# Two matrix mixes in one program: the second mix also takes the first one's banks and tiles in the last ten steps

## The chip, the cores and the metric

The kernel runs on one core of a Trainium2 chip. The core's engines work side by side, each through its own queue, in order: TensorE (PE; its weight loads are listed as PEld), VectorE (DVE), ScalarE (ACT), GpSimd (POOL), and SyncE (SP), which here issues the DMAs. Matrix products land in PSUM, which the kernel uses as eight tiles of 128 x 512 floats, called banks below; everything else lies in SBUF. The metric is the device time of one execution in microseconds (us).

## What is computed

Three layers on an input of 2 batch rows x 4160 tokens x 192 channels, all in 32-bit floats, cut to what matters:

```python
w = softmax(weight_gen)                          # 8 heads, 7 taps
x = einsum('bshk,bskhg->bshg', w, windows(x))    # causal window of 7 tokens
# first mix ("moe"): 192 -> 1024 -> 192
xk = mu_k * x + (1 - mu_k) * x_prev
xr = mu_r * x + (1 - mu_r) * x_prev
k = maximum(xk @ w_k, 0)
x = sigmoid(xr @ w_r) * ((k * k) @ w_v)
# second mix ("moe2"): 192 -> 1024 -> 192
h = maximum(x @ w_in, 0)
conv = sum over k of conv_w[k] * h shifted by k - 1    # 3 taps along the tokens
out = (h * sigmoid(conv)) @ w_out
```

## The kernel before

The tokens are cut into ten tiles (`SIZES`: 256, 248, seven of 472, and 352), and a tile is worked on for both batch rows. The hidden width of 1024 is cut into `NF = 8` chunks of 128, which stand on the partitions. Channels 0 to 127 and 128 to 191 are kept in two parts, and each operand as a high and a low part, so that a product of full accuracy is made of five matmuls.

**A step of the first mix** (`moe1`) is one chunk of one tile and batch row: five matmuls into a bank `pa`, Relu and Square in place, a high part copied to `s` (ACT), the low part (DVE), and five matmuls with `wv` that add up in the banks `am` and `ar`. When the eight chunks are done, `mix_out` multiplies by the gate and writes the result to `x2[b]`, the second mix's input.

**A step of the second mix** (`moe2`, L623) is, for one chunk:

- `go`: five matmuls of `x2[b]` with `wiA` and `wiB` into a bank `pc` (5 passes of N + 2 columns);
- `c1`: Relu from the bank to a tile `h` (ACT); `c2`: `h` times the middle tap back into the bank (ACT);
- two taps on DVE, each a SCALAR_TENSOR_TENSOR that adds to the bank; `c5`: Sigmoid in the bank (ACT); `c6`: `h` times the bank into the bank (DVE), called the product;
- `c7`: the high part from the bank to a tile `g` (ACT); `c8`: the low part, bank minus high part, to `g` (DVE);
- `go2`: five matmuls of `g` with `wo` that add up in `bm` and `br`, called the sums. After chunk 7, `store` copies `bm` to `om` and a part of `br` to `ob` (ACT), adds the rest on DVE, and sends both out.

**Who has how many buffers.** Two banks each for `pa` and `pc`, one each for `am`, `ar`, `bm`, `br`: all eight. Two tiles each of `s`, `g`, `h`, and of `mk`, which the blending with the previous token uses (`mixing`). A `Ring` hands its tiles out in turn. A step of the second mix holds its bank from `go` to `c8`, `h` from `c1` to `c6`, and `g` from `c7` to `go2`.

**What sets the order.** Each piece of work is recorded with a due time (`at`): tile i starts at T = 16 i, batch row 1 eight later, `moe1` of chunk fi at T + fi, and `moe2` ten (`LAG`) behind it. `Program.schedule` (L99) plays the recorded operations through, with the costs of `cost` (L72): at each moment an engine takes, of the operations whose inputs and buffers are ready, the one with the earliest due time. The instructions are then issued in the order of the starts so found. A ring's choice is made before, in the order of the due times, so that a buffer is bound to a step when the step is recorded, and a reuse becomes a dependence that the order obeys. The first mix's last step is due at 159 to 160.25, the second mix's last one at 169.5 to 171.75.

In the trace all instructions bear one line (L167), since `schedule` issues them all; operations are told apart by tile names and by engine. The last tile has 352 tokens; its second mix works on 354 or 356 columns.

Of the kernel before, what the change touches and what calls it, by code (L numbers as in the profile page):

```python
# [16 lines left out]
NTILE = len(SIZES)  # L17
# [7 lines left out]
WIN = KS * DM  # L25
NF = DFF // 128
LAG = 10


def f(ap):  # L30
    return ap.bitcast(F32)


class Program:
# [3 lines left out]
    def __init__(self, nc):  # L38
        self.ops, self.spaces = [], {}
        self.real = {"PE": nc.tensor, "ACT": nc.scalar, "DVE": nc.vector, "POOL": nc.gpsimd, "SP": nc.sync}  # L40
# [129 lines left out]
class Ring:  # L170
# [5 lines left out]
    def __call__(self):  # L176
        self.n += 1
        return self.tiles[(self.n - 1) % len(self.tiles)]
# [3 lines left out]
def conv_moe_kernel(ctx: ExitStack, tc: tile.TileContext, xp, wg_first, wg_rest, mus, w_k, w_v, w_r, w_in, conv_w, w_out, out):  # L182
    nc = tc.nc
    prog = Program(nc)
# [4 lines left out]
    def new(name, shape, dtype=F32):  # L189
        t = sb.tile(shape, dtype, name=name)  # L190
        prog.spaces[t.tensor.name] = "SBUF"
        return t

    def ring(name, n, shape, dtype=F32):
        return Ring([new(f"{name}{j}", shape, dtype) for j in range(n)])

    def bank(name):
        t = ps.tile([128, 512], F32, name=name)
        prog.spaces[t.tensor.name] = "PSUM"
        return t  # L200

    W = NMAX + 4

    mu = new("mu", [128, 4])
    onemu = new("onemu", [128, 4])
    cw = new("cw", [128, 3, NF])
# [21 lines left out]
    mk_r = ring("mk", 2, [128, NMAX])  # L228
# [4 lines left out]
    s_r = ring("s", 2, [128, 2, NMAX], F32R)  # L233
    g_r = ring("g", 2, [128, 2, W], F32R)
    h_r = ring("h", 2, [128, W])
# [14 lines left out]
    pa_r = Ring([bank(f"pa{j}") for j in range(2)])  # L250
    pc_r = Ring([bank(f"pc{j}") for j in range(2)])
    am_r, ar_r, bm_r, br_r = (Ring([bank(x)]) for x in ("am", "ar", "bm", "br"))

    px_r = Ring([bm_r.tiles[0], br_r.tiles[0]])
    py_r = Ring(pc_r.tiles)

    plan = []

    def at(t, fn, hold=0.0):
        plan.append((t, len(plan), fn, hold))  # L260

    def mm(dst, passes):
        n = len(passes)
        for i, (w, r) in enumerate(passes):
            PE.matmul(dst, lhsT=w, rhs=r, start=(i == 0), stop=(i == n - 1))
# [262 lines left out]
    def moe1(i, b, fi, t):  # L528
        N = SIZES[i]
        st = {}  # L530
        sl = slice(128 * fi, 128 * fi + 128)

        def go():
            p = pa_r()
            st["p"] = p[:, :N]
            mm(st["p"], passes_in(wkA, wkB, xin[i, b, 0, 0], xin[i, b, 0, 1], sl, N))

        def c1():
            ACT.activation(st["p"], st["p"], ACTF.Relu)

        def c2():
            ACT.activation(st["p"], st["p"], ACTF.Square)

        def c3():
            s = s_r()
            st["s"] = s
            ACT.copy(s[:, 0, :N], st["p"])

        def c4():
            s = st["s"]  # L550
            DVE.tensor_tensor(s[:, 1, :N], st["p"], f(s[:, 0, :N]), op=ALU.subtract)

        def go2():
            if fi == 0:
                acc["m"] = am_r.tiles[0]
                acc["r"] = ar_r.tiles[0]
            out_passes(wv, fi, st["s"], N, acc["m"], acc["r"])

        at(t, go)
        at(t + 0.28, c1)  # L560
        at(t + 0.45, c2)
        at(t + 0.56, c3)
        at(t + 0.68, c4)
        at(t + 1.25, go2)

    def out_passes(W, fi, s, n, am, ar):
        s0, s1 = s[:, 0, :n], s[:, 1, :n]
        a, z = fi == 0, fi == NF - 1
        PE.matmul(am[:, :n], lhsT=W[:, fi, 0], rhs=s0, start=a, stop=False)
        PE.matmul(am[:, :n], lhsT=W[:, fi, 1], rhs=s0, start=False, stop=False)  # L570
        PE.matmul(ar[:, :n], lhsT=W[:, fi, 2], rhs=s0, start=a, stop=False)
        PE.matmul(am[:, :n], lhsT=W[:, fi, 0], rhs=s1, start=False, stop=z)
        PE.matmul(ar[:, :n], lhsT=W[:, fi, 2], rhs=s1, start=False, stop=z)
# [13 lines left out]
    def mix_out(i, b, t):  # L587
        N = SIZES[i]
        X = x2[b]
        c = slice(2, N + 2)  # L590
        m, r = am_r.tiles[0], ar_r.tiles[0]

        def d0():
            DVE.tensor_tensor(m[:, :N], r_t[0][:, :N], m[:, :N], op=ALU.mult)

        def d1():
            DVE.tensor_tensor(r[:, :N], r_t[1][:, :N], r[:, :N], op=ALU.mult)

        def a0():
            ACT.copy(X[:, 0, c], m[:, :N])  # L600

        def a1():
            ACT.copy(X[:, 2, c], r[:, :N])
            ACT.copy(X[0:64, 3, c], r[0:64, :N])

        def d2():
            DVE.tensor_tensor(X[:, 1, c], m[:, :N], f(X[:, 0, c]), op=ALU.subtract)

        def d3():
            DVE.tensor_tensor(X[64:128, 3, c], r[0:64, :N], f(X[0:64, 2, c]), op=ALU.subtract)  # L610

        at(t, d1)
        at(t + 0.14, d0)
        at(t + 0.15, a1)
        at(t + 0.3, a0)
        at(t + 0.4, d3)
        at(t + 0.5, d2)
# [5 lines left out]
    def moe2(i, b, fi, t):  # L623
        last = i == NTILE - 1
        N = SIZES[i] + (2 if last else 0)
        X = x2[b]
        st = {}
        sl = slice(128 * fi, 128 * fi + 128)

        def go():  # L630
            p = pc_r()
            st["p"] = p
            n = N + 2
            mm(p[:, :n], [(wiA[:, 0, sl], X[:, 0, :n]), (wiA[:, 1, sl], X[:, 0, :n]), (wiA[:, 0, sl], X[:, 1, :n]),
                          (wiB[:, 0, sl], X[:, 2, :n]), (wiB[:, 1, sl], X[:, 3, :n])])

        def c1():
            h = h_r()
            st["h"] = h
            ACT.activation(h[:, :N + 2], st["p"][:, :N + 2], ACTF.Relu)  # L640

        def c2():
            ACT.activation(st["p"][:, :N], st["h"][:, 1:N + 1], ACTF.Copy, scale=cw[:, 1, fi:fi + 1])

        def tap(k, o):
            DVE.scalar_tensor_tensor(out=st["p"][:, :N], in0=st["h"][:, o:o + N], scalar=cw[:, k, fi:fi + 1],
                                     in1=st["p"][:, :N], op0=ALU.mult, op1=ALU.add)

        def c5():
            ACT.activation(st["p"][:, :N], st["p"][:, :N], ACTF.Sigmoid)  # L650

        def c6():
            DVE.tensor_tensor(st["p"][:, :N], st["h"][:, 1:N + 1], st["p"][:, :N], op=ALU.mult)

        def c7():
            g = g_r()
            st["g"] = g
            ACT.copy(g[:, 0, :N], st["p"][:, :N])

        def c8():  # L660
            g = st["g"]
            DVE.tensor_tensor(g[:, 1, :N], st["p"][:, :N], f(g[:, 0, :N]), op=ALU.subtract)

        def go2():
            if fi == 0:
                acc2["m"] = bm_r()
                acc2["r"] = br_r()
            out_passes(wo, fi, st["g"], N, acc2["m"], acc2["r"])

        at(t + 0.5, go)  # L670
        at(t + 0.78, c1)
        at(t + 0.9, c2)
        at(t + 1.03, lambda: tap(0, 0))
        at(t + 1.17, lambda: tap(2, 2))
        at(t + 1.35, c5)
        at(t + 1.47, c6)
        at(t + 1.66, c7)
        at(t + 1.8, c8)
        at(t + 2.75, go2)

    def store(i, b, t):
        N = SIZES[i]
        last = i == NTILE - 1
        a = 1 if i == 0 else 0
        n = N + (1 if last else 0)
        t0 = STARTS[i] - 1
        st = {}

        def e0():
            st["b"] = ob_r()  # L690
            ACT.copy(st["b"][:, :n], acc2["r"][64:128, :n])

        def e1():
            st["m"] = om_r()
            ACT.copy(st["m"][:, :n], acc2["m"][:, :n])
            SP.dma_start(out=out[b, 0:128, t0 + a:t0 + n], in_=st["m"][:, a:n])

        def e2():
            DVE.tensor_tensor(st["b"][:, :n], acc2["r"][0:64, :n], st["b"][:, :n], op=ALU.add)
            SP.dma_start(out=out[b, 128:192, t0 + a:t0 + n], in_=st["b"][:, a:n])  # L700

        at(t, e0)
        at(t + 0.1, e1)
        at(t + 0.2, e2)
# [36 lines left out]
    for i in range(NTILE):  # L741
# [6 lines left out]
        for b in range(NB):  # L748
# [4 lines left out]
            for fi in range(NF):  # L753
                moe1(i, b, fi, t + fi)
                moe2(i, b, fi, t + fi + LAG)
            mix_out(i, b, t + 8.52)
            store(i, b, t + LAG + 10.02)

# [68 lines left out]
```

## Time and profile before

| | us |
|---|---|
| median of 3 runs | 791.23 (789.27 to 791.41) |
| the profiled execution | 793.36 |
| its span, first to last instruction | 791.6 |
| busy in the span: PE, DVE, ACT, POOL | 697.2, 631.4, 666.5, 506.2 |

PE is busy 88% of the span, and the share is not even: in the middle of the program PE is full, at both ends it isn't. An engine's busy time by itself doesn't tell what bounds a stretch. Read by stretch instead which engine is full there, and, where none is, who waits for whom. In the rows below a timeline gives start and duration of an instruction, and in brackets how long its engine was idle before it and what ended that. The duration runs to the end of the result; the next instruction of the same engine can start before that, so an engine's pace is read from the starts of neighbours.

### The profile page before, as it was taken

The page shows a single profiled execution, that of the slowest core. Times are in us where ns is not written, and L with a number is a line of the kernel's source. Part 1 is how long each engine was busy: PE and PEld are TensorE (multiplying, and loading weights), DVE is VectorE, ACT ScalarE, POOL GpSimd, SP SyncE. Part 2 cuts the span into 40 slices and gives each one's busy share as a digit, 9 for nine tenths or more (in the row PEclk, how much of TensorE's full clock was granted, in tenths as well). Part 3 has the DMA queues.
Part 4 walks back from the last instruction along what each step waited for, and adds up shares of the span by engine and source line. Part 5 has one row for each costly group of instructions (what it writes and reads, how often), then busy time and mean ns, then how long its engine had stood idle before and what let it go on. Part 6 is the DMA issues. An engine that isn't in the chain of part 4 may idle for free.

```text
span 791.6 us, 10781 instructions
## 1 busy us (share of the span) xinstructions
PE 697.2 (88%) x3505; PEld 607.3 (77%) x3505; DVE 631.4 (80%) x1137; ACT 666.5 (84%) x1441; POOL 506.2 (64%) x368
## 2 busy tenths in 40 slices
PE   0066776999999999999999999999999999999964
PEld 0054675898888888888888888888888888889843
DVE  5987977887878787878877887879787878788764
ACT  2467798998989899989898989989898989899854
POOL 5898888899999999999999789295401101000000
PEclk9997786999999999999999999999999999999998
DMA  7685010130130112112121211020002000100000
GB/s 202 194 277 174 13 51 11 58 103 10 61 99 19 51 69 59 59 51 91 28 69 51 68 46 58 7 68 1 20 12 56 20 1 21 35 19 1 20 14 14
DMA packets 19241, 45.09 MB, mean 57 GB/s; under 512 B 3057, under 2 KB 14705, under 8 KB 19057
## 3 DMA queue, kind: packets, MB, share of 16 engines
q1 hardware_dynamic: 19184, 44.41, 18.9%
q8 instruction: 27, 0.44, 0.2%
q14 instruction: 30, 0.24, 0.1%
HBM read 27.40 MB, written 6.39 MB: 43 GB/s over the span
## 4 chain that ended last, share of the span: by engine, by line
PE 68%; ACT 15%; DVE 13%; issue 2%; DMA 2%; SPq 0%; ACTq 0%; DVEq 0%
PE pa L167 21%; PE pc L167 16%; PE am L167 10%; PE bm L167 9%; PE ar L167 7%; PE br L167 5%; DVE pc L167 4%; ACT pa L167 2%; ACT pc L167 2%; DVE stage L167 2%; ACT h L167 2%; ACT g L167 2%; ACT L167 1%; DMA stage<-in_moe_w_k_dram 1%; DVE bm L167 1%
## 5 line engine op out<-in xcount | busy, mean ns | idle before, releaser
L167 DVE SCALAR_TENSOR_TENSOR pc<-h,cw,pc 128x472 f32<-128x472 f32 (+3 forms) x320 | 208.1, 650 | 39.5 <-ACT pc L167 36.7
L167 POOL TENSOR_TENSOR prod<-rows,sw 128x1344 f32<-128x1344 f32 x70 | 216.1, 3087 | 12.8 <-DMA rows<-in_x_dram 7.8
L167 ACT ACTIVATE pa<-pa 128x472 f32<-128x472 f32 (+3 forms) x320 | 160.8, 505 | 39.1 <-PE pa L167 35.2
L167 POOL TENSOR_TENSOR prod<-prod 128x576 f32<-128x576 f32 (+1 forms) x140 | 171.0, 1221 | 8.6
L167 PE MATMUL bm<-g,wo 128*128 128x472 f32 (+3 forms) x480 | 148.7, 360 | 21.3 <-ACT g L167 21.1
L167 PE MATMUL am<-s,wv 128*128 128x472 f32 (+3 forms) x480 | 147.0, 367 | 7.1 <-ACT s L167 5.8
L167 DVE TENSOR_TENSOR pc<-h,pc 128x472 f32<-128x472 f32 (+3 forms) x160 | 94.7, 592 | 59.2 <-ACT pc L167 57.9
L167 PE MATMUL pa<-xA,wkA 128*128 128x472 f32 (+3 forms) x480 | 125.9, 368 | 7.5 <-DVE s L167 3.4
L167 PE MATMUL pc<-x,wiA 128*128 128x474 f32 (+3 forms) x480 | 121.6, 361 | 3.5 <-DVE g L167 3.5
L167 POOL TENSOR_TENSOR xA<-mk,xA 128x472 fp32r<-128x472 f32 (+2 forms) x36 | 40.4, 1128 | 123.1 <-ACT xA L167 96.6
L167 PE MATMUL ar<-s,wv 128*128 128x472 f32 (+3 forms) x320 | 112.6, 364 | 4.9 <-DVE x L167 3.3
L167 PEld LDWEIGHTS bm<-g,wo 128*128 128x128 f32 x480 | 88.3, 191 | 35.4 <-ACT g L167 26.0
L167 PE MATMUL br<-g,wo 128*128 128x472 f32 (+3 forms) x320 | 112.4, 355 | 1.4 <-DVE ob L167 1.4
L167 DVE TENSOR_TENSOR s<-pa,s 128x472 fp32r<-128x472 f32 (+3 forms) x160 | 93.7, 586 | 16.8 <-ACT s L167 15.8
L167 DVE TENSOR_TENSOR g<-pc,g 128x472 fp32r<-128x472 f32 (+3 forms) x160 | 93.8, 586 | 15.5 <-ACT g L167 14.0
L167 PEld LDWEIGHTS am<-s,wv 128*128 128x128 f32 x480 | 89.1, 197 | 21.4 <-ACT s L167 11.0
L167 PEld LDWEIGHTS pa<-xA,wkA 128*128 128x128 f32 x480 | 87.6, 199 | 19.9 <-DVE s L167 6.4
L167 ACT ACTIVATE pc<-h,cw 128x472 f32<-128x472 f32 (+3 forms) x160 | 99.7, 623 | 1.8
L167 PEld LDWEIGHTS pc<-x,wiA 128*128 128x128 f32 x480 | 85.7, 193 | 15.9 <-DVE g L167 5.8
L167 ACT ACTIVATE h<-pc 128x474 f32<-128x474 f32 (+3 forms) x160 | 84.4, 527 | 11.4 <-PE pc L167 8.3
L167 ACT ACTIVATE pc<-pc 128x472 f32<-128x472 f32 (+3 forms) x160 | 80.9, 506 | 14.0 <-DVE pc L167 13.0
L167 PE MATMUL pa<-xB,wkB 128*128 128x472 f32 (+3 forms) x320 | 89.8, 362 | 1.5 <-DMA xB<-mk 1.5
(105 smaller groups left out, 1066.4 us busy)
## 6 DMA issues: line engine op xcount, KB each, us to landing
rows<-in_x_dram SPq DMA_DIRECT2D x14, 960.0 KB, 4.5
xB<-rm SPq DMA_DIRECT2D x28, 118.0 KB, 2.3
xB<-mk SPq DMA_DIRECT2D x28, 118.0 KB, 2.3
out_dram<-om SPq DMA_DIRECT2D x14, 236.0 KB, 2.0
rows<-in_x_dram SPq DMA_DIRECT2D x4, 768.0 KB, 7.1
rows<-in_x_dram SPq DMA_DIRECT2D x2, 864.0 KB, 4.5
out_dram<-ob SPq DMA_DIRECT2D x14, 118.0 KB, 2.2
stage<-in_moe_w_v_dram SPq DMA_DIRECT2D x4, 384.0 KB, 3.9
```

The lines of the kernel that those rows point to most:

```text
L167: getattr(self.real[eng], method)(*a, **k)
```

## The change

A new class `Shift` is a ring with two sets of tiles: its own and lent ones. With `since`, it hands out its own tiles in turn until the due time `since`, and from then on own and lent ones in turn, beginning with the own one whose turn it is. Three such rings take the place of `pc_r`, `h_r` and `g_r` in `moe2`: the banks `pa` are lent to `pc`, the tiles `mk` to `h`, and the tiles `s` to `g`, all from the due time `DONE` = 160.3 on, when the first mix has no work left. Of the second mix, ten steps have their `go` due at or behind that: chunks 6 and 7 of batch row 0 and all eight of batch row 1 in the last tile (high parts are due later in a step, so that `g` has eleven). No operation is added or removed; the scheduler plays the new dependences through and finds a new order.

```diff
+DONE = 16 * NTILE + 0.3
...
+    class Shift:
+        def __init__(self, own, lent, till=None, since=None):
+            self.both, self.own, self.tiles, self.till, self.since = Ring(own + lent), Ring(own), own, till, since
+
+        def __call__(self):
+            if self.since is None:
+                return self.both() if prog.now < self.till else self.own()
+            if prog.now < self.since:
+                return self.own()
+            if not self.both.n:
+                k = self.own.n % len(self.tiles)
+                self.both.tiles = self.tiles[k:] + self.tiles[:k] + self.both.tiles[len(self.tiles):]
+            return self.both()
...
+    pt_r = Shift(pc_r.tiles, pa_r.tiles, since=DONE)
+    ht_r = Shift(h_r.tiles, mk_r.tiles, since=DONE)
+    gt_r = Shift(g_r.tiles, s_r.tiles, since=DONE)
...
         def go():
-            p = pc_r()
+            p = pt_r()
...
         def c1():
-            h = h_r()
+            h = ht_r()
...
         def c7():
-            g = g_r()
+            g = gt_r()
```

In the rows of the order, `pa_111` and `pa_112` are the banks pa0 and pa1, `pc_113` and `pc_114` are pc0 and pc1, `h_103`, `h_104`, `mk_83`, `mk_84`, `g_101`, `g_102`, `s_99` and `s_100` the tiles 0 and 1 of their rings, and `x_0_73` and `x_1_74` the second mix's input of batch row 0 and 1. All rows up to these places read the same in both programs.

PE, from where the first mix's last matmuls are over; before:

```order
L167 MATMUL bm<-g_102,wo 128x354 x2
L167 MATMUL br<-g_102,wo 128x354
L167 MATMUL pc_114<-x_0_73,wiA 128x356 x3
L167 MATMUL pc_114<-x_0_73,wiB 128x356 x2
L167 MATMUL bm<-g_102,wo 128x354
L167 MATMUL br<-g_102,wo 128x354
L167 MATMUL bm<-g_101,wo 128x354 x2
L167 MATMUL br<-g_101,wo 128x354
L167 MATMUL pc_113<-x_1_74,wiA 128x356 x3
```

and now:

```order
L169 MATMUL pa_111<-x_1_74,wiA 128x356 x2
L169 MATMUL pa_112<-x_1_74,wiA 128x356 x2
L169 MATMUL pa_111<-x_1_74,wiA 128x356
L169 MATMUL pa_111<-x_1_74,wiB 128x356
L169 MATMUL pa_112<-x_1_74,wiA 128x356
L169 MATMUL pa_111<-x_1_74,wiB 128x356
L169 MATMUL pa_112<-x_1_74,wiB 128x356 x2
L169 MATMUL bm<-g_102,wo 128x354 x2
L169 MATMUL br<-g_102,wo 128x354
L169 MATMUL pc_114<-x_0_73,wiA 128x356 x3
L169 MATMUL pc_114<-x_0_73,wiB 128x356 x2
```

The first two steps of batch row 1 now stand ahead of the last step of batch row 0, in the lent banks, and ahead of the sums of its chunk 5.

DVE at the same place, behind the last instruction that makes `x_1`; before:

```order
L167 TENSOR_TENSOR pc_114<-h_104,pc_114 128x354
L167 SCALAR_TENSOR_TENSOR pc_113<-h_103,cw,pc_113 128x354
L167 TENSOR_TENSOR g_102<-pc_114,g_102 128x354
L167 SCALAR_TENSOR_TENSOR pc_113<-h_103,cw,pc_113 128x354
L167 TENSOR_TENSOR pc_113<-h_103,pc_113 128x354
L167 SCALAR_TENSOR_TENSOR pc_114<-h_104,cw,pc_114 128x354
L167 TENSOR_TENSOR g_101<-pc_113,g_101 128x354
L167 SCALAR_TENSOR_TENSOR pc_114<-h_104,cw,pc_114 128x354
L167 TENSOR_TENSOR pc_114<-h_104,pc_114 128x354
```

and now:

```order
L169 TENSOR_TENSOR pc_114<-h_104,pc_114 128x354
L169 SCALAR_TENSOR_TENSOR pc_113<-h_103,cw,pc_113 128x354 x2
L169 TENSOR_TENSOR g_102<-pc_114,g_102 128x354
L169 SCALAR_TENSOR_TENSOR pa_111<-mk_83,cw,pa_111 128x354
L169 TENSOR_TENSOR pc_113<-h_103,pc_113 128x354
L169 SCALAR_TENSOR_TENSOR pa_111<-mk_83,cw,pa_111 128x354
L169 SCALAR_TENSOR_TENSOR pa_112<-mk_84,cw,pa_112 128x354
L169 TENSOR_TENSOR g_101<-pc_113,g_101 128x354
L169 TENSOR_TENSOR pa_111<-mk_83,pa_111 128x354
L169 SCALAR_TENSOR_TENSOR pc_114<-h_104,cw,pc_114 128x354
L169 SCALAR_TENSOR_TENSOR pa_112<-mk_84,cw,pa_112 128x354
```

Before, work of two steps alternates; now that of three or four steps is interleaved.

DVE at the end of the program; before:

```order
L167 SCALAR_TENSOR_TENSOR pc_114<-h_104,cw,pc_114 128x354
L167 TENSOR_TENSOR g_101<-pc_113,g_101 128x354
L167 SCALAR_TENSOR_TENSOR pc_114<-h_104,cw,pc_114 128x354
L167 TENSOR_TENSOR pc_114<-h_104,pc_114 128x354
L167 TENSOR_TENSOR g_102<-pc_114,g_102 128x354
L167 TENSOR_TENSOR ob_106<-br,ob_106 64x353
```

and now, from the low part that frees the last step's bank:

```order
L169 TENSOR_TENSOR s_99<-pc_114,s_99 128x354
L169 TENSOR_TENSOR pa_112<-mk_84,pa_112 128x354
L169 SCALAR_TENSOR_TENSOR pc_113<-h_103,cw,pc_113 128x354
L169 TENSOR_TENSOR g_102<-pa_112,g_102 128x354
L169 TENSOR_TENSOR pc_113<-h_103,pc_113 128x354
L169 TENSOR_TENSOR g_101<-pc_113,g_101 128x354
L169 SCALAR_TENSOR_TENSOR pc_114<-h_104,cw,pc_114 128x354 x2
L169 TENSOR_TENSOR pc_114<-h_104,pc_114 128x354
L169 TENSOR_TENSOR s_99<-pc_114,s_99 128x354
L169 TENSOR_TENSOR ob_106<-br,ob_106 64x353
```

The last step's two taps, which had another step's low part between them, now follow each other directly.

## Rows read from the trace of the kernel before

**Rows 1.** Busy us by stretch: PE, PEld, DVE, ACT, POOL; granted clock; DMA.
```profile
740.00:750.00 10.00, 10.00 (x63) 9.85 (x62) 7.60 (x16) 8.41 (x21) 0.00 (x0) 1.00 0.01 3
750.00:760.00 10.00, 5.33 (x29) 4.10 (x27) 7.34 (x16) 6.59 (x15) 0.00 (x0) 1.00 0.00 0
770.00:780.00 10.00, 6.37 (x31) 4.85 (x32) 6.29 (x14) 5.58 (x12) 0.00 (x0) 1.00 0.00 0
```

**Rows 2.** Waits from 749 us on: us in total, times, longest.
```profile
PE bm L167 <- ACT g L167: 13.5, 10, 2.2
DVE pc L167 <- ACT pc L167: 10.6, 17, 0.9
```

**Rows 3.** Timeline of PE: start, us, operation, count, [idle before <- releaser].
```profile
753.44 0.59 PE L167 MATMUL bm<-g,wo 128*128 128x354 f32 x2 [2.23 <-ACT g L167]
753.87 0.33 PE L167 MATMUL br<-g,wo 128*128 128x354 f32 x1
754.03 0.72 PE L167 MATMUL pc<-x,wiA 128*128 128x356 f32 x3
...
770.68 0.76 PE L167 MATMUL pc<-x,wiA 128*128 128x356 f32 x3
...
777.26 0.75 PE L167 MATMUL pc<-x,wiA 128*128 128x356 f32 x3
...
786.49 0.58 PE L167 MATMUL bm<-g,wo 128*128 128x354 f32 x1
```

**Rows 4.** Timeline of ACT, same columns.
```profile
747.75 0.47 ACT L167 CAST s<-pa 128x352 fp32r<-128x352 f32 x1
748.10 0.50 ACT L167 ACTIVATE h<-pc 128x356 f32<-128x356 f32 x1
...
771.81 0.47 ACT L167 ACTIVATE h<-pc 128x356 f32<-128x356 f32 x1 [0.20 <-PE pc L167]
772.31 0.56 ACT L167 ACTIVATE pc<-h,cw 128x354 f32<-128x354 f32 x1
772.80 0.45 ACT L167 CAST g<-pc 128x354 fp32r<-128x354 f32 x1
774.45 0.45 ACT L167 ACTIVATE pc<-pc 128x354 f32<-128x354 f32 x1 [1.20 <-DVE pc L167]
```

**Rows 5.** Timeline of DVE, same columns.
```profile
752.39 0.51 DVE L167 TENSOR_TENSOR pc<-h,pc 128x354 f32<-128x354 f32 x1
...
763.67 1.22 DVE L167 SCALAR_TENSOR_TENSOR pc<-h,cw,pc 128x354 f32<-128x354 f32 x2
...
772.90 0.59 DVE L167 SCALAR_TENSOR_TENSOR pc<-h,cw,pc 128x354 f32<-128x354 f32 x1 [0.72 <-ACT pc L167]
773.40 0.52 DVE L167 TENSOR_TENSOR g<-pc,g 128x354 fp32r<-128x354 f32 x1
773.84 0.58 DVE L167 SCALAR_TENSOR_TENSOR pc<-h,cw,pc 128x354 f32<-128x354 f32 x1
...
776.68 0.52 DVE L167 TENSOR_TENSOR g<-pc,g 128x354 fp32r<-128x354 f32 x1
...
783.68 0.58 DVE L167 SCALAR_TENSOR_TENSOR pc<-h,cw,pc 128x354 f32<-128x354 f32 x1
...
788.07 0.52 DVE L167 TENSOR_TENSOR ob<-br,ob 64x353 f32<-64x353 f32 x1 [1.72 <-ACT ob L167]
```

**Rows 6.** Timeline of SP, which issues the stores.
```profile
788.62 0.47 SPq L167 DMA_DIRECT2D out_dram<-ob  x1
```

**Rows 7.** Two early stretches, columns as in rows 1.
```profile
120.80:124.20 3.40, 1.08 (x9) 0.98 (x9) 3.25 (x7) 2.34 (x7) 2.55 (x3) 1.00 0.00 0
124.20:127.60 3.40, 2.89 (x14) 2.60 (x13) 2.19 (x5) 3.34 (x6) 2.13 (x3) 0.50 0.00 0
```

**Rows 8.** Timeline of PE at half clock, columns as in rows 3.
```profile
118.79 0.41 PE L167 MATMUL bm<-g,wo 128*128 128x256 f32 x1
119.00 0.41 PE L167 MATMUL br<-g,wo 128*128 128x256 f32 x1
```

## The prediction

> **What bounds the kernel now.** I read the busy time by stretch first. Up to 750 us TensorE (PE) is busy 10.00 of 10 us; in the stretch 750 to 760 only 5.33, and in 770 to 780 only 6.37, and there no other engine is full either: VectorE (DVE) has 7.34 and 6.29, ScalarE (ACT) 6.59 and 5.58 [rows 1]. From about 750 us, then, a chain of latencies sets the pace, not an engine. The waits of that end say which: PE's output matmuls wait 13.5 us for ACT's g, DVE waits 10.6 us for ACT over the bank pc [rows 2]. The rows of one step show the chain, and the reader should see it go from engine to engine: matmuls into a bank from 770.68 [rows 3], Relu 771.81, scaled copy 772.31 [rows 4], first tap 772.90, second tap 773.84 [rows 5], Sigmoid 774.45 [rows 4], then the product and the high part, low part 776.68 [rows 5], and only then the next matmuls into the same bank, 777.26 [rows 3]. That is 6.58 us for a bank, and with two banks one step in 3.29 us.
>
> I call the steps of the second mix A0 to A7 (batch row 0) and B0 to B7 (batch row 1), by hidden chunk; the last ten are A6, A7 and B0 to B7. They take the end from DVE's product of step A5 at 752.39 to DVE's last instruction at 788.07 + 0.52 = 788.59 [rows 5]: 36.2 of 791.6 us.
>
> **The change, part by part.** No instruction is added or removed. Up to DVE's product of A5 all engines have the old order, so the first 752.39 us stay. Behind it the ten steps go over four banks in turn: A6 pc0, A7 pc1, B0 pa0, B1 pa1, and so on; B7 has pc1, which B3 had. With h (mk0, mk1) and the products (s0, s1) it is the same.
>
> *What a step costs each engine when nothing waits.* DVE's pace is read from starts of neighbours: tap to low part 772.90 to 773.40, 0.50; low part to tap 773.40 to 773.84, 0.44 [rows 5]. A step has two taps and two tensor operations: 2 x 0.50 + 2 x 0.44 = 1.88 us. ACT's is 0.35 for a plain copy (747.75 to 748.10) and 0.49 for the scaled one (772.31 to 772.80) [rows 4]: with Relu, Sigmoid and high part taken as plain ones, 3 x 0.35 + 0.49 = 1.54. PE's is 0.16 a matmul (753.87 to 754.03) [rows 3]: 10 x 0.16 = 1.6. The chain, over four banks, allows 6.58 / 4 = 1.65. DVE's 1.88 is the largest, so DVE becomes the engine that sets the pace: 1.88 in place of 3.29.
>
> *What ends last.* B7 can't start before B3 has left pc1. In the new order of DVE, B3's low part is the 34th instruction, counted from the product of A5: 17 taps and 17 tensor operations, 17 x 0.50 + 17 x 0.44 = 15.98 us. To that come waits. I walked the new orders of DVE, ACT and PE row by row: an instruction starts at its neighbour's start plus the pace, or 0.02 us (PE: 0.05) behind the end of what it waits for, whichever is later. In these 34 DVE stands still seven times, 0.64 us in all; the longest are 0.17, before the product of A6 (its Sigmoid comes late in ACT's queue), and 0.13. So B3's low part ends at 752.39 + 15.98 + 0.64 + 0.09 = 769.10 (0.09, since it lasts 0.53 and the pace is 0.44). In PE's queue 12 matmuls follow that end up to the last one into B7's bank: two of B3's sums, five of B4's, five of B7. The first has to load its weights behind the wait and takes 0.27 instead of 0.16 (753.44, two before 753.87) [rows 3]. 769.15 + 0.27 + 10 x 0.16 + 0.33 = 771.35, and 0.04 later Relu could start. The walk has it at 771.54, since ACT's copy of B6's high part stands before it; I take 771.5.
>
> From there on B7 runs alone, as the last step does now. Relu to first tap is 1.09 (771.81 [rows 4] to 772.90 [rows 5]). Now a low part of another step stands between the taps (772.90, 773.40, 773.84); in the new order the two taps follow each other, 0.61 apart (two in 1.22) [rows 5]. From the last step's second tap at 783.68 to the end of DVE's last sum at 788.59 are 4.91 [rows 5]. 1.09 + 0.61 + 4.91 = 6.61, and 771.54 + 6.61 = 778.15.
>
> **The sum:** 788.59 - 778.15 = 10.44 us less. What comes behind, the last store, issued at 788.62 [rows 6], and its 3.0 us to the end of the span, stays. The span goes from 791.6 to 781.2, the profiled execution from 793.36 to 782.9, and the median of the runs, 791.23 (2.1 below the profiled one), to 780.8. As a trial, the same walk over the old order ends at 788.0 where the trace has 788.59; part of these 0.6 us are PE's last matmuls, one of 0.58 [rows 3] where 0.33 is usual; the walk has them at full pace.
>
> *Operands that the trace doesn't show in this form:* the taps and products read mk and pa in place of h and pc. Same shape, same memories; ACT's copy into s took 0.47 and into g 0.45 [rows 4]. Bound: 0 to 0.02 us for 15 copies, nothing that shows, since ACT has room.
>
> *Waits that the loans add:* pa0 and pa1 wait for the first mix's last low parts, which stand ahead of A5's product in DVE's order; mk waits for the copies to xB, and the first mix has used xB to the end by then. Both cost nothing. The matmuls of B0 and B1 stand ahead of A5's sums in PE's queue and wait there for x_1. In the walk A5's sums so start at 753.92 in place of 753.44; it is paid back, because PE is idle 2.23 us there now [rows 3] and DVE has work. The sums of B0 wait for the store of batch row 0 (bm, br and ob exist once); in the walk bm is read out by 763.46, B0's sums end at 764.62, and s1, which they free, is wanted again at 765.96. If the read-out came over 1.3 us later, ACT and then DVE would stand still.
>
> *PE's clock.* The granted clock is full (1.00) in the stretch 750 to 760, at 53% busy, and in 770 to 780 [rows 1]. Earlier a stretch with 1.08 of 3.40 us busy was followed by one at 0.50 [rows 7]. In the walk PE is busy 17 of the 25.5 us from 751.1 to 776.6, 67%, more than now; the sum takes the full clock, 2.4 GHz. The Trainium skill (TensorE: Matmul & The Clock Gate, section "Part 1: The HAM clock gate") says that the throttled state is the default and that only activity lifts it. Both stretches here agree with that; read strictly it would allow a fall wherever PE pauses, and by it the time would be that of the third rival below.
>
> **Rivals.** *One: ACT and DVE hold each other up more than in the walk.* In 740 to 750, where four banks are in use by the two mixes, DVE is busy only 7.60 of 10 us [rows 1]. With that share the 34 instructions take 15.98 / 0.76 = 21.0 us in place of 16.62: 4.4 more, 785.2 us. Against it: in that stretch PE is full, here it isn't.
>
> *Two: the change doesn't do what it says.* If something keeps only two steps under way (the single bm and br, or a wait on the first mix), each step still takes 3.29 us: 791.2. For it: batch row 1 may not be summed before the store. Against it: the order has the matmuls of B0 to B3 ahead of the first sum of B0.
>
> *Three, slower: the clock falls at the end of the first mix and stays down.* At half clock (0.50, 1.2 GHz) matmuls of 256 columns start 0.21 apart (118.79 to 119.00) [rows 8]; for 354 columns I take 0.21 x 354 / 256 = 0.29. From 751 on there are 50 + 55 = 105 matmuls; 105 x (0.29 - 0.16) = 13.7 us, so 794.5 if every one lies on the path. It decides from 80 of the 105 on: 80 x 0.13 = 10.4, the whole gain. For it: pauses of 1.7 and 2.5 us that the walk gives PE near 767 and 773. Against it: ten pauses of up to 2.2 us now, 13.5 us together [rows 2], under a full clock, and DVE's slack hides part of the price.
>
> **How the numbers follow.** Forecast 780.8: 0.80. Rival one, 785.2: 0.14. Rival two, 791.2: 0.03. Rival three, 794.5: 0.03. Range: below, the fastest run of before, 789.27, less 10.44, is 778.8; I take 778.6. Above, DVE's share of 96% in the walk (15.98 of 16.62) may sink to 0.82, a little under half of the way to rival one: 19.5 us, 2.9 more, 783.7. About 0.8 lies within. 0.3% of 791.23 is 2.4 us, about what a measurement of this kernel can tell from no change; the forecast and rival one are beyond it: faster 0.94, same 0.03, slower 0.03.
>
> **What would show it.** Right: DVE's product of A5 again at 752.4; from there to 770 DVE busy over 90%, one step in about 1.9 us; Relu of B7 near 771.5; the last sum near 778.2; store and span end 3.0 us later; clock at 1.00 up to there. Wrong: DVE's product of A5 at another time (then the start isn't the same); idle pieces of DVE over 0.3 us before 769 (rival one); PE's sums of B0 waiting long for ob (rival two); matmuls of 356 columns 0.29 apart between 752 and 772 (rival three).

## The result

| | before | after |
|---|---|---|
| median, us | 791.12 (789.27 to 791.41, 4 runs) | 780.34 (779.78 to 781.87, 4 runs) |
| span of the profiled execution | 791.6 | 778.5 |
| from DVE's product of A5 to the end of its last sum, "the tail" | 36.20 | 25.75 |

The time is 0.9873 of before, 95% interval 0.9857 to 0.989: 10.8 us less, where 10.4 were forecast, 780.34 where 780.8 were. The spans of the two profiled executions differ by 13.1 us, though. The tail accounts for 10.45 of that; 2.62 lie ahead of A5's product, which stands at 752.39 before [rows 5] and at 749.77 after, although DVE and ACT have the same instructions up to there, and PE has them up to 748.43. All of the 2.62 is there by 150 us, long ahead of the change: PE's first matmul starts at 15.43 before and 13.64 after, its 451st at 149.61 and 146.99. In the fourteen profiles of this study A5's product stands between 748.05 and 752.39: that is the scatter of single executions, and the profile of before was the slowest of them. So a variant is judged here by its tail, inside one profile, and by its median.

### The profile page after: what moved, and what is told of

Read it like the earlier page. It is cut to its first block, busy times and chain, and to the rows that moved or that the text cites. A ratio compares the mean times of both kernels' runs of the same rounds, so it can differ in the third digit from the quotient of the medians.

```text
span 778.5 us, 10782 instructions
## 1 busy us (share of the span) xinstructions
PE 694.1 (89%) x3505; PEld 606.3 (78%) x3505; DVE 630.8 (81%) x1137; ACT 665.5 (85%) x1441; POOL 506.6 (65%) x368
## 4 chain that ended last, share of the span: by engine, by line
PE 68%; ACT 14%; DVE 14%; issue 2%; DMA 1%; SPq 0%; ACTq 0%; DVEq 0%
PE pa L169 21%; PE pc L169 16%; PE am L169 10%; PE bm L169 9%; PE ar L169 7%; PE br L169 6%; DVE pc L169 4%; ACT pa L169 2%; DVE stage L169 2%; ACT pc L169 2%; ACT h L169 2%; ACT g L169 2%; ACT L169 1%; DVE bm L169 1%; DVE s L169 1%
## 5 line engine op out<-in xcount | busy, mean ns | idle before, releaser
L169 DVE SCALAR_TENSOR_TENSOR pc<-h,cw,pc 128x472 f32<-128x472 f32 (+3 forms) x312 | 203.7, 653 | 34.9 <-ACT pc L169 31.9
L169 ACT ACTIVATE pa<-pa 128x472 f32<-128x472 f32 (+3 forms) x324 | 162.7, 504 | 37.9 <-PE pa L169 33.8
L169 PE MATMUL bm<-g,wo 128*128 128x472 f32 (+3 forms) x465 | 144.5, 361 | 9.6 <-ACT g L169 9.0
L169 DVE TENSOR_TENSOR pc<-h,pc 128x472 f32<-128x472 f32 (+3 forms) x156 | 92.6, 594 | 54.4 <-ACT pc L169 53.0
L169 PE MATMUL pc<-x,wiA 128*128 128x474 f32 (+3 forms) x468 | 118.6, 361 | 3.2 <-DVE g L169 3.2
L169 PE MATMUL br<-g,wo 128*128 128x472 f32 (+3 forms) x310 | 109.4, 356 | 0.0
L169 DVE TENSOR_TENSOR g<-pc,g 128x472 fp32r<-128x472 f32 (+3 forms) x153 | 90.4, 591 | 16.4 <-ACT g L169 14.9
L169 ACT ACTIVATE pc<-h,cw 128x472 f32<-128x472 f32 (+3 forms) x156 | 97.5, 625 | 1.6
L169 ACT ACTIVATE h<-pc 128x474 f32<-128x474 f32 (+3 forms) x156 | 82.5, 529 | 9.6 <-PE pc L169 7.5
L169 PE MATMUL pc<-x,wiB 128*128 128x474 f32 (+3 forms) x312 | 87.4, 359 | 0.0
```

What stands on the lines that cost most here:

```text
L169: getattr(self.real[eng], method)(*a, **k)
```

## The profile after

The busy time by stretch, columns as in rows 1 (busy us with instructions of PE, PEld, DVE, ACT and POOL, then the granted clock):

```profile
750.00:760.00 10.00, 7.67 (x39) 5.95 (x39) 9.93 (x21) 8.43 (x21) 0.00 (x0) 1.00 0.00 1
760.00:770.00 10.00, 8.45 (x50) 7.65 (x49) 8.89 (x19) 8.08 (x20) 0.00 (x0) 1.00 0.09 27
770.00:778.50 8.50, 1.77 (x9) 1.09 (x8) 2.76 (x5) 1.98 (x5) 0.00 (x0) 0.78 0.11 32
```

In the first row DVE has 9.93 of 10 where it had 7.34 [rows 1]: an engine has taken the place of the chain as the bound. The last row is nearly the last step alone, and the clock falls only at its end. The waits from 749 us on, as in rows 2:

```profile
PE bm L169 <- ACT s L169: 4.4, 3, 2.4
ACT pc L169 <- DVE pc L169: 1.6, 2, 1.3
...
DVE pc L169 <- ACT pc L169: 0.9, 2, 0.5
```

DVE's wait for ACT over pc has gone from 10.6 us to 0.9. PE waited ten times for ACT's high part, 13.5 us in all; now it waits four times, 5.0 us, of which the three over `s` make 4.4. The timeline of DVE has the forecast's marks: the product of A5, three neighbours that give its paces, the low part of B3 that frees the last bank, the two taps of B7, and the last sum.

```profile
749.77 0.51 DVE L169 TENSOR_TENSOR pc<-h,pc 128x354 f32<-128x354 f32 x1
750.20 1.20 DVE L169 SCALAR_TENSOR_TENSOR pc<-h,cw,pc 128x354 f32<-128x354 f32 x2
...
757.63 0.58 DVE L169 SCALAR_TENSOR_TENSOR pc<-h,cw,pc 128x354 f32<-128x354 f32 x1
758.12 0.52 DVE L169 TENSOR_TENSOR g<-pa,g 128x354 fp32r<-128x354 f32 x1
758.55 0.52 DVE L169 TENSOR_TENSOR s<-pc,s 128x354 fp32r<-128x354 f32 x1
...
761.76 0.53 DVE L169 TENSOR_TENSOR g<-pc,g 128x354 fp32r<-128x354 f32 x1 [0.18 <-ACT g L169]
...
766.21 0.52 DVE L169 TENSOR_TENSOR s<-pc,s 128x354 fp32r<-128x354 f32 x1
...
770.20 1.22 DVE L169 SCALAR_TENSOR_TENSOR pc<-h,cw,pc 128x354 f32<-128x354 f32 x2 [0.43 <-ACT pc L169]
...
775.00 0.52 DVE L169 TENSOR_TENSOR ob<-br,ob 64x353 f32<-64x353 f32 x1 [1.48 <-ACT ob L169]
```

The 0.18 at 761.76 is the only idle piece that the view marks between the product and B3's low part. B7's Relu, on ACT, and the last matmuls of the program, on PE:

```profile
769.10 0.47 ACT L169 ACTIVATE h<-pc 128x356 f32<-128x356 f32 x1
```

```profile
773.60 0.39 PE L169 MATMUL bm<-s,wo 128*128 128x354 f32 x1
773.84 0.32 PE L169 MATMUL br<-s,wo 128*128 128x354 f32 x1
```

The last matmuls take 0.39 and 0.32 where before one took 0.58 [rows 3]: the clock fell at 774.84, behind them. Columns as in rows 1:

```profile
770.00:774.84 4.84, 1.77 (x9) 1.09 (x8) 2.24 (x4) 1.85 (x5) 0.00 (x0) 1.00 0.00 0
774.84:778.50 3.66, 0.00 (x0) 0.00 (x0) 0.52 (x1) 0.12 (x1) 0.00 (x0) 0.50 0.25 74
```

## The experiments

Each kernel is timed against the kernel before. "Walk" is the row-by-row walk of the prediction over the kernel's own order; "with clock" is the same walk with matmuls at half pace (0.29 us for 354 columns) in the pieces in which the trace shows a granted clock of 0.50 (1.2 GHz, the lower of its two levels; 1.00 is 2.4 GHz). For the kernel after the walk ends at 25.3; the forecast, 36.20 - 10.44 = 25.76, took the end of the last step from rows of before instead.

| run | tail, us | walk | walk with clock | median | ratio, 95% interval |
|---|---|---|---|---|---|
| before | 36.20 | 35.5 | 35.5 | | |
| after | 25.75 | 25.3 | 25.3 | 780.34 | 0.9873 (0.9857 to 0.989) |
| banks_only | 26.92 | 26.3 | 26.3 | 781.04 | 0.9881 (0.9864 to 0.9897) |
| tiles_only | 36.62 | 35.5 | 35.7 | 789.88 | 0.9991 (0.998 to 1.0001) |
| banks_h | 26.54 | 25.5 | 25.8 | 780.27 | 0.9866 (0.985 to 0.9883) |
| six_banks | 23.30 | 23.0 | 23.0 | 777.46 | 0.9837 (0.9822 to 0.9851) |
| six_only | 27.52 | 26.3 | 26.8 | 782.08 | 0.9897 (0.9865 to 0.9929) |
| dve_load_after | 30.48 | 28.5 | 30.1 | 783.64 | 0.9915 (0.9901 to 0.993) |
| dve_load_before | 38.62 | 36.7 | 38.1 | 791.49 | 1.0018 (1.0006 to 1.0029) |
| act_load_after | 30.45 | 26.9 | 30.1 | 784.17 | 0.9922 (0.9905 to 0.9938) |
| act_load_before | 37.52 | 35.5 | 36.8 | 792.2 | 1.003 (1.0015 to 1.0045) |
| dve_load_fill | 29.83 | 28.8 | 29.5 | 783.62 | 0.9917 (0.9888 to 0.9945) |
| act_load_fill | 28.33 | 27.3 | 27.9 | 782.5 | 0.9909 (0.9879 to 0.9938) |
| less_pe | 27.75 | 25.0 | 27.6 | 782.54 | 0.9897 (0.9866 to 0.9929) |

### Which of the loans counts

banks_only takes the loans of `h` and `g` back:

```diff
-            h = ht_r()
+            h = h_r()
...
-            g = gt_r()
+            g = g_r()
```

> Only the banks pa are lent; h and g keep their two tiles. The tail is counted from DVE's product of step A5 to the end of DVE's last sum: 36.20 us before, 25.75 with all three loans. Theory (a step holds its bank for 6.6 us and that alone limits how many are under way; h and g are held for about half of it): most of the gain stays, the walk over the new order of rows gives a tail about 1.0 us longer than with all loans, 26.7 to 27.0, and 781.4 us. Rival (four banks need four tiles of h and g): tail 32 or more, 787 us or more.

The tail is 26.92, so 9.28 of the 10.45 us come from the two banks alone. What the tiles add, 1.2 us, the medians can't tell apart. tiles_only is the other half, `p = pc_r()` in place of `pt_r()`:

> Only the tiles mk and s are lent to h and g; the steps keep two banks. Theory (the banks alone limit): the order differs only in tile names, tail 36.2, 791.1 us, no change. Rival (h and g hold steps up as well): tail 34 or less, 789 us or less.

No change in the median (the interval holds 1). Its tail is 0.4 longer than before's, and its clock fell 3 us ahead of the end. The first row is A5's product, the second the last sum, in the timeline of DVE of tiles_only:

```profile
748.54 0.51 DVE L169 TENSOR_TENSOR pc<-h,pc 128x354 f32<-128x354 f32 x1
...
784.65 0.52 DVE L169 TENSOR_TENSOR ob<-br,ob 64x353 f32<-64x353 f32 x1 [2.04 <-ACT ob L169]
```

banks_h lends banks and `mk`, and keeps `g = g_r()`:

> The banks and mk are lent, s isn't. Theory: g is held only from the high part to the sums, two tiles are enough; tail 25.8 to 26.0, 780.5 us, as with all three loans. Rival (the sums of batch row 1 wait for the store of batch row 0, and with two g the steps stop behind that): tail 27.5 or more, 782 us or more.

The tail was 26.54, between the two forecasts. The clock explains 0.3 of the excess (it fell 2.6 us ahead of the last sum's start; the walk goes from 25.5 to 25.8). The median is that of the full change. So the loan of `s` to `g` is worth less than a microsecond here, and whether it is worth anything is open.

### How many banks

six_banks lends `am` and `ar` too, which `mix_out` has read out by then:

```diff
-    pt_r = Shift(pc_r.tiles, pa_r.tiles, since=DONE)
+    pt_r = Shift(pc_r.tiles, pa_r.tiles + am_r.tiles + ar_r.tiles, since=DONE)
```

> All three loans, and the banks am and ar as well, which the first mix has left by then: six banks. Theory (DVE sets the pace until B6, and the last step runs alone only since it waits for the bank of B3): the pace stays at DVE's, but B7 no longer runs alone at the end; the walk gives a tail 2.4 us shorter, 23.3 to 23.6, and 778.0 us. Rival (the end is a chain that no bank shortens): tail 25.7, 780.3 us.

The tail is 23.30, at the lower end of what was expected, and the kernel is faster than the changed one: 777.46 us, an interval that ends at 0.9851, below the 0.9857 at which the changed kernel's begins. The timeline of DVE near the end shows why:

```profile
768.03 1.08 DVE L169 SCALAR_TENSOR_TENSOR pa<-h,cw,pa 128x354 f32<-128x354 f32 x2
769.02 0.52 DVE L169 TENSOR_TENSOR g<-pc,g 128x354 fp32r<-128x354 f32 x1
769.46 0.96 DVE L169 TENSOR_TENSOR pa<-h,pa 128x354 f32<-128x354 f32 x2
770.56 0.53 DVE L169 TENSOR_TENSOR g<-pa,g 128x354 fp32r<-128x354 f32 x1
771.00 0.52 DVE L169 TENSOR_TENSOR s<-pa,s 128x354 fp32r<-128x354 f32 x1
773.38 0.52 DVE L169 TENSOR_TENSOR ob<-br,ob 64x353 f32<-64x353 f32 x1 [1.86 <-ACT ob L169]
```

B6 and B7 now go through DVE side by side ("x2" joins an operation of each) without an idle piece that the view marks: the last step no longer waits for a bank. What is left behind DVE's last low part is the sums, the copies and the store. six_only keeps the six banks and takes the loans of `h` and `g` back:

> Six banks (pa, am and ar lent) as in six_banks, but h and g keep their two tiles. Theory (with four banks the tiles hardly matter, since h and g are held for about half of the time that a bank is; with six banks more steps are under way than two h allow): the loan of banks gives nothing beyond four, walk 26.3, tail 26.5 to 27.0, 781.1 us, as banks_only. Rival (banks alone limit, whatever their number): 23.3 to 24, 777.7 us, as six_banks.

The tail is 27.52, longer than banks_only's 26.92; 0.5 of it is the clock, which fell at 772.1, 7 us ahead of the end. So the rival is out: two tiles each of `h` and `g` are about enough for four banks, and too few for six. Which buffer limits is a question of the number of steps under way, not a property of the buffer.

### Which engine sets the pace

One more operation in each of the last ten steps, whose result nobody reads; dve_load_after adds a product to DVE (shown), act_load_after in its place a copy, `ACT.copy(att_r()[:, :N], st["p"][:, :N])`, to ACT, and the two others add the same to the kernel before:

```diff
+        def extra():
+            if prog.now >= 16 * NTILE + 1.3:
+                DVE.tensor_tensor(att_r()[:, :N], st["h"][:, 1:N + 1], st["p"][:, :N], op=ALU.mult)
+
+        at(t + 1.5, extra)
```

> The changed kernel with one more DVE operation in each of the last ten steps, behind the product: h times the bank into a tile that nobody reads, 0.44 us of DVE each. Theory (DVE sets the pace from A5 to B6): each shows in the time as long as DVE is full; at most 10 x 0.44 = 4.4, the walk gives 3.2, since the last ones find DVE waiting: tail 28.9, 783.5 us. Rival (the chain of a step over four banks or ACT sets the pace): 1 us or less, tail under 26.8.

> The kernel before with the same ten operations on DVE. Theory (there a bank is held for 6.6 us and DVE has slack): little shows, the walk gives 1.1 (part of them delay a tap of the other step): tail 37.3, 792.2 us. Rival (DVE was the limit before as well): 3 to 4.4 us, tail 39 to 40.6.

> The changed kernel with one more copy on ACT in each of the last ten steps, from the bank into a tile that nobody reads, 0.35 us of ACT each. Theory (DVE at 1.88 us a step sets the pace, ACT has 1.54): 0.34 us a step are free, so of 3.5 us the walk lets 1.5 show, where ACT's queue makes DVE wait: tail 27.3, 781.9 us. Rival (ACT sets the pace as much as DVE): 3 us or more, tail 28.8 or more.

> The kernel before with the same ten copies on ACT. Theory: ACT waits for DVE in each step and has room; tail 36.2, 791.1 us. Rival: the copies stand ahead of work on the chain and each shows, tail 38 or more.

All four tails came out longer than expected, by 1.3 to 3.2 us, and act_load_after went past the mark that I had set for the rival. In each of them PE's clock was down for a piece of the tail. In these rows of act_load_after, columns as in rows 1, PE has pauses in the first and third stretch, and in the second and fourth the granted clock is 0.50:

```profile
756.50:759.90 3.40, 1.10 (x6) 0.81 (x6) 2.88 (x8) 2.75 (x8) 0.00 (x0) 1.00 0.00 0
759.90:763.30 3.40, 3.40 (x12) 3.40 (x12) 2.65 (x5) 2.59 (x7) 0.00 (x0) 0.50 0.06 22
766.70:770.10 3.40, 1.74 (x11) 1.32 (x10) 2.65 (x7) 3.09 (x8) 0.00 (x0) 1.00 0.00 0
770.10:773.50 3.40, 3.40 (x13) 3.40 (x12) 1.86 (x4) 1.48 (x4) 0.00 (x0) 0.50 0.00 0
```

At 12 and 13 matmuls in 3.4 us, PE is full there: 0.26 to 0.28 us each, about the price of rival three. With the pieces at half clock put into the walk, it comes within 0.3 to 0.7 us of all four traces. What the load itself costs is then the difference of the walks without clock: DVE's 3.2 us after and 1.2 before, ACT's 1.6 after and none before.

But the load need not be what brought the clock down. In the two loads on the kernel before, the first fall, at 749.7 in both, stands ahead of the first added operation (751.96, and 753.47 in act_load_before). The first two rows are dve_load_before around its fall, the third is the kernel before at the same place, columns as in rows 1; below them stand the first matmul behind PE's pause and the first added product in dve_load_before:

```profile
746.30:749.70 3.40, 1.35 (x9) 1.05 (x7) 3.31 (x8) 2.76 (x7) 0.00 (x0) 1.00 0.00 0
749.70:753.10 3.40, 3.23 (x10) 2.87 (x10) 2.20 (x5) 1.02 (x3) 0.00 (x0) 0.50 0.00 0
749.85:753.25 3.40, 1.36 (x9) 1.07 (x7) 3.30 (x8) 2.73 (x7) 0.00 (x0) 1.00 0.00 0
```

```profile
749.87 0.96 PE L167 MATMUL bm<-g,wo 128*128 128x354 f32 x2 [2.23 <-ACT g L167]
...
751.96 0.52 DVE L167 TENSOR_TENSOR att<-h,pc 128x354 f32<-128x354 f32 x1
```

The kernel before has the same instructions up to there and the same pause of 2.23 us [rows 3], and its clock stayed at 1.00 for another 33 us. So one program can meet a fall at this place in one execution and none in another. The loads on the changed kernel are another case: the mean granted clock of a whole execution stands on record for every run, and it is 0.967 or 0.968 in all four of act_load_after and 0.969 or 0.970 in those of dve_load_after, against 0.972 to 0.974 in those of the changed kernel, so there the lower clock is not that of one profile alone. In dve_load_before it is 0.970 in the profiled run and one more, and 0.972 in the other eight.

That the surplus is the clock was my reading, not yet shown; so two runs added a matmul to each step, behind its sums, into the bank `am` (eleven in all, since A5's sums are due late enough to get one too):

```diff
+        def fill():
+            if prog.now >= 16 * NTILE + 1.3:
+                PE.matmul(am_r.tiles[0][:, :N], lhsT=wo[:, fi, 0], rhs=st["g"][:, 0, :N], start=True, stop=True)
+        at(t + 2.8, fill)
```

> As act_load_after (one more copy on ACT in each of the last ten steps), with the same added matmul. In act_load_after the clock fell twice before the end (759.9 to 763.3 and 770.1 to 773.5), behind 1.10 and 1.74 of 3.4 us busy; tail 30.45, walk 26.9 without the falls and 30.1 with them. Theory (DVE sets the pace, ACT's load by itself costs 1.5 us, and the rest was the clock): 27.7 if PE keeps the clock, 29.2 if it falls once, and in each case within 0.7 of the walk with the falls that the trace then shows. Rival (ACT sets the pace as much as DVE): 30 or more with the clock at 1.00.

With more work the tail fell from 30.45 to 28.33, within 0.7 of the walk with the fall (27.9) as expected, and the clock stayed at 1.00 to 774.1, 3.4 us ahead of the end. So ACT's load costs 28.33 - 25.75 = 2.6 us with the added matmul and the late fall in it, not 4.7, out of the 10 x 0.35 = 3.5 that were added. But the added matmul did not work as I had thought. In the same place the pause is as long as before, and the clock stays:

```profile
755.50:758.90 3.40, 1.07 (x5) 0.78 (x5) 2.95 (x7) 2.77 (x9) 0.00 (x0) 1.00 0.00 0
758.90:762.30 3.40, 3.32 (x20) 3.29 (x21) 2.98 (x6) 3.35 (x10) 0.00 (x0) 1.00 0.15 53
```

1.07 of 3.40 us without a fall, 1.10 with one: the pause alone doesn't decide, and whether the added matmuls kept the clock or the pause only came at a luckier moment is open. In its four runs the mean granted clock is 0.970 to 0.973, above act_load_after's, but the ratios' intervals overlap.

> As dve_load_after (one more DVE operation in each of the last ten steps), and behind each step's sums one more matmul of 354 columns into the bank am, which nobody reads. In dve_load_after the granted clock fell to 0.50 from 758.7 to 762.1, behind a stretch in which PE was busy 1.92 of 3.4 us; the tail was 30.48, the walk without a fall has 28.5 and with it 30.05. Theory (the surplus of 1.6 us is the clock): with a little more work PE keeps the full clock, and the tail gets shorter although work was added: the walk has 28.8, so 29.0 to 29.4, 782.2 us. Rival (the surplus is DVE's or ACT's queueing, and PE is near its limit): 30.5 or more, 783.7 us or more.

A half miss: the clock stayed at 1.00 through the middle, but fell at 772.3, 5.6 us ahead of the end, so that the tail is 29.83, 0.65 shorter than without the added matmuls and not 1.1 to 1.5. The median, 783.62, is that of dve_load_after. The load of ten DVE operations costs 29.83 - 25.75 = 4.1 us, again with the added matmul and the late fall in it, where ten times their pace are 4.4. By the walks the late falls make 0.7 of this and 0.6 of ACT's 2.6. That leaves about 3.4 of 4.4 us for DVE and 2.0 of 3.5 for ACT: DVE sets the pace more than ACT does, but ACT comes close behind. In the 16.96 us of the changed kernel from 749.77 to 766.73, DVE is busy 16.56 and ACT 14.60.

The clean test takes PE work away. In the last ten steps less_pe leaves out two of the ten matmuls of each step:

```diff
+        if less:
+            PE.matmul(ar[:, :n], lhsT=W[:, fi, 2], rhs=s0, start=a, stop=False)
+            PE.matmul(am[:, :n], lhsT=W[:, fi, 0], rhs=s1, start=False, stop=z)
+            PE.matmul(ar[:, :n], lhsT=W[:, fi, 2], rhs=s1, start=False, stop=z)
+            return
         PE.matmul(am[:, :n], lhsT=W[:, fi, 1], rhs=s0, start=False, stop=False)
...
-            mm(p[:, :n], [(wiA[:, 0, sl], X[:, 0, :n]), (wiA[:, 1, sl], X[:, 0, :n]), (wiA[:, 0, sl], X[:, 1, :n]),
+            some = [(wiA[:, 1, sl], X[:, 0, :n])] if i < NTILE - 1 or b == 0 and fi < 6 else []
+            mm(p[:, :n], [(wiA[:, 0, sl], X[:, 0, :n])] + some + [(wiA[:, 0, sl], X[:, 1, :n]),
```

> The changed kernel; the last ten steps leave out two of their ten matmuls each (the low part of w_in times the high part of x, and the low part of w_out times the high part of g). 20 matmuls of 0.16 us less work on PE, 3.2 us. Theory (DVE sets the pace, and PE's pauses are near those behind which the clock fell in the runs with load): at a full clock the tail hardly moves, walk 25.0, so 25.4; if the clock falls, the tail is longer than the 25.75 of the changed kernel although work was taken away, 26.5 to 28. Rival (PE's matmuls are on the path): 24.5 or less.

The tail is 27.75, 2.0 us longer than the changed kernel's with 20 matmuls less, and the median 782.54, 2.2 us above it, all four runs between 781.43 and 782.88. The intervals of the two ratios overlap, so the median alone would not show it. The mean granted clock is 0.967 to 0.972 in its four runs, none above the lowest of the changed kernel's. Its profile has two falls, in the second and fourth of these stretches:

```profile
754.00:757.40 3.40, 1.83 (x8) 1.24 (x8) 3.40 (x9) 2.45 (x7) 0.00 (x0) 1.00 0.00 0
757.40:760.80 3.40, 2.89 (x10) 2.89 (x11) 2.75 (x7) 2.13 (x6) 0.00 (x0) 0.50 0.00 0
764.30:767.70 3.40, 1.72 (x9) 1.23 (x8) 3.40 (x9) 3.06 (x8) 0.00 (x0) 0.99 0.00 0
767.70:771.10 3.40, 3.08 (x11) 2.92 (x11) 2.82 (x6) 1.10 (x3) 0.00 (x0) 0.50 0.00 0
```

DVE, full at 3.40 in the first and third stretch, falls to 2.75 and 2.82 where the clock is down, and there PE, at 2.89 and 3.08, is the busier of the two. Its matmuls start 0.30 and 0.29 apart in these rows of PE, inside the second stretch:

```profile
758.67 0.50 PE L169 MATMUL bm<-s,wo 128*128 128x354 f32 x1
758.97 0.50 PE L169 MATMUL br<-s,wo 128*128 128x354 f32 x1
759.26 0.80 PE L169 MATMUL pa<-x,wiB 128*128 128x356 f32 x2
```

The walk has 25.0 without the falls and 27.6 with them: with 20 matmuls less and a full clock the tail would have been no longer than the changed kernel's.

## Why the prediction was right

**The start.** DVE and ACT do the same up to A5's product, as forecast. PE doesn't quite: its first matmuls for B0 start at 748.43, 1.34 us ahead of the product, and hold nothing up, since from A4's low part to the product DVE takes 3.43 us (from 746.34) where it took 3.41. The product's place moved by 2.62 us, and the prediction had named that as a sign of being wrong. It isn't one here: the shift is complete by 150 us, 600 us ahead of the first changed instruction.

**The pace.** DVE's paces held to a hundredth: 757.63 to 758.12 is 0.49 for a tap, 758.12 to 758.55 is 0.43 for a tensor operation, where 0.50 and 0.44 were taken. B3's low part ends at 766.73, 16.96 behind A5's product, where 16.71 were forecast (15.98 of work, 0.64 of standing still, 0.09). At the forecast's paces DVE so stood still for 0.89, a quarter of a microsecond more than in the walk; at the paces read here the work is 17 x 0.92 = 15.64 and the standing still 1.23. Two terms, each some tenths off, offset each other in part.

**The start of B7.** Relu at 769.10, 19.33 behind the product; the forecast had 19.15. As in the walk, ACT's copy of B6's high part stands just ahead of it.

**B7 alone.** 6.42 us from its Relu to the end of the last sum, forecast 6.61. Here the term was too large by the slow matmuls of before: I took the last 4.91 us over as they stood, with the clock falling in them [rows 3]; after, it fell behind them. This error of 0.19 and the one of 0.18 ahead of it cancel, so that the sum, 10.44 against 10.45, agrees to 0.01 is luck; its terms agree to about 0.2.

**The rivals.** One: DVE is busy 9.93 of 10 us, and 16.56 of the 16.96 up to the end of B3's low part, not 76%; out. Two: out by the same row. tiles_only shows what it would have looked like, had the loan missed the buffer that limits. Three, the clock, I priced rightly (0.29 to 0.30 against 0.29 us a matmul), but gave it only the form "down to the end", with 0.03. The runs show the likelier form: single pieces of half clock, each worth 1.3 to 1.6 us by the walks. The profile of the changed kernel had none before its end; variants that differ from it by one small operation a step had one or two, and the kernel before with a load had one ahead of any added operation. So the forecast held by less room than its chances said.

## What to carry to other kernels

Where no engine is full, look for the buffer that is held longest by one piece of work; its hold time over the number of buffers is the pace, and only more of that buffer help, until the next limit (here the busiest engine, then the next buffer) comes up. Count what other stages have left behind at the end of a program: all banks that are free, not those of one ring, gave another 2.9 us in the median and 2.5 in the tail. And judge such an edit by a stretch inside one profile, since the same code ahead of it moved by 4 us between executions; look at the granted clock of that stretch first, since one program met a fall in one execution and none in another.

## What the runs showed of the hardware

That TensorE's clock would cost time in a stretch where it was busy half to two thirds of the time was not expected. With less PE work the tail was longer (less_pe, 27.75 us with two falls, against 25.75), and with a load on ACT alone the clock fell twice in 14 us (act_load_after). In the pieces at half clock, matmuls of 354 columns were 0.29 to 0.30 apart instead of 0.16. The kernel before, with steady pauses of 1.2 us, kept the full clock for 33 us. The Trainium skill (TensorE: Matmul & The Clock Gate, section "Part 1: The HAM clock gate") says that activity releases the throttle; less_pe, with its 20 matmuls less, agrees with that. What no run here tells is at which moment a pause counts. The sharpest case is one and the same list of instructions: behind a pause of 2.23 us, with PE busy 1.35 of 3.40 us, the clock fell in dve_load_before, and behind the same pause, with 1.36 of 3.40, it did not in the kernel before.
